# Reordering a top-k attention and mixer kernel: exps ahead of score copies in the second batch, mixing and a last exp moved earlier in the first

## The chip, the cores and the metric

The kernel runs on one core of a Trainium2 chip. The metric is the device time of one execution in microseconds. Three runs of the kernel before took 1866.98, 1867.06 and 1869.12 us, with a median of 1867.06 us; lower is better. The profiled execution of it spans 1865.9 us from its first to its last instruction.

The engines are named as the profile names them: PE is the matrix engine (PEld its weight loads), DVE the vector engine, ACT the scalar engine, POOL the general engine, SP the engine that issues most of the loads and stores.

## The reference

For each of 8 batches and 8 heads, 576 queries attend to 576 keys with head size 64, but only the 32 largest scores of each row are kept. The attention output, with heads side by side, is then the input `x` (576 rows of 512) of a mixer: a low-rank mixing along the sequence, then a two-layer network along the channels.

```python
scores = scale * np.matmul(q, k.transpose(0, 1, 3, 2))
kth = np.partition(scores, -top_k, axis=-1)[..., -top_k:-top_k + 1]
scores = np.where(scores >= kth, scores, -1000000000.0)
attn = np.exp(scores - np.max(scores, axis=-1, keepdims=True))
attn = attn / (np.sum(attn, axis=-1, keepdims=True) + 1e-09)
x = attn @ v                                   # (B, H, S, D) -> (B, S, H*D)

h = x.transpose(0, 2, 1) @ U @ V               # rank 32, along the sequence
u = x + h.transpose(0, 2, 1)
out = u + np.maximum(u @ w_ch1, 0.0) @ w_ch2   # 512 -> 2048 -> 512
```

## The kernel before

Heads are taken in pairs: 4 pairs in a batch, 32 pairs in all. The 576 rows of a pair are cut into four tiles of 128 rows and a tail of 64 rows (both heads of the pair share the tail's tile). A **step** is one tile of one pair, so a pair has 5 steps (`t` = 0 to 4, 4 being the tail), the first batch has steps 0 to 19, the second has steps 20 to 39, and there are 160 steps. Every tile but the tail has two chunks of 128 rows x 576 scores, one for each head; the tail has one.

The order of the instructions on PE, ACT, DVE and POOL is the order in which this program emits them, and each engine works through its own in that order. The program spreads the parts of a step over later steps with Python generators; each `next(...)` emits the part up to the next `yield`.

What becomes of one tile `(g, t)`:

```python
def scores(g, t):              # PE: q times k into PSUM; ACT: three copies out of it into Ssb
    ...
    copy(main[:, :, 0:HALF], scs[0][:, :, 0:HALF])                             # L303
    nc.scalar.copy(main[:, :, HALF:MAIN], scs[1][:, :, 0 : MAIN - HALF])       # L304
    nc.scalar.copy(last, scs[1][:, :, MAIN - HALF : HALF])                     # L305

def front(g, t):               # the top-k and the exps
    ...                        # DVE: first 8 maxima of each chunk (L337)
    yield
    for i in range(1, TOPK // 8):
        if i == 1:
            nc.scalar.mul(nmax[:, 0:n], first[:, 0:n, 0], -SCALE)              # L344
            for c in early:                 # not "eased": exps here already
                weigh(chunks[c], Es[c], nmax[:, c : c + 1])
        ...                    # DVE: match_replace (L349) and max (L353), each chunk
        yield
    if pooled:                 # POOL: scores of chunk 1 under the 32nd get a huge negative number
        nc.gpsimd.tensor_scalar(Es[1], chunks[1], ms[1][:, 7:8], NEG, ALU.is_lt, ALU.mult)   # L356
        nc.gpsimd.tensor_tensor(chunks[1], chunks[1], Es[1], ALU.add)                        # L357
    for c in early:            # DVE: zero what lies under the 32nd, and sum (L359)
        nc.vector.scalar_tensor_tensor(...)
    yield
    if ease:                   # the same for chunk 0 by ACT (L373, L374) and POOL (L375)
        nc.scalar.mul(least, ms[0][:, 7:8], WIDEN)
        nc.scalar.activation(Es[0], chunks[0], AF.Relu, bias=least, scale=-WIDEN)
        nc.gpsimd.tensor_tensor(chunks[0], chunks[0], Es[0], ALU.subtract)
        yield
    for c in order:            # (1, 0)
        if c not in early:
            weigh(chunks[c], Es[c], nmax[:, c : c + 1], sums[c])               # ACT exp, L310
    ...
    yield

def turns(g, t):               # PE transposes E (L395, L400), ACT copies into PT (L396, L401)
def values(g, t):              # PE: PT times v (L429, L432; tail L419), ACT copies into XT (L441)
def mixed(g, wait):            # PE transposes XT, ACT copies to x (L457), POOL divides (L458);
                               # after `wait` calls: PE times U (L464), ACT copies to Tb (L472);
                               # PE times V (L476, L478), ACT copies to uT (L486), in two parts
```

A step is *eased* when `ease` holds: the first two batches' tiles other than tails (and other than step 18). `fill()` emits one call of a `mixed` generator if one is under way, and then a share of the two-layer network's matmuls (`mlp`, PE L501 and L520), once a batch's `mixed` generators are all done; in the first batch there is therefore no such filling. The first batch's steps also decode the parameters (`next_params`: ACT L165 to L168, DVE L175, POOL L176 and L178), and so does the first half of the second batch.

The step loop, second batch and later (`n >= ALONE + 1`; `ease` is that of step n - 1, `last` its generator, `here` that of step n):

```python
        if ease:
            next(last, None)               # least, Relu (ACT), subtract (POOL) of step n - 1
        fill()
        next(turning, None)                # rest of turns(n - 2)
        fill()
        next(turning, None)
        fill()
        next(ready, None)                  # a part of prep: the next pair's q and k
        fill()
        if n - 2 >= ALONE:
            values(*divmod(n - 2, CH))
        if n + 1 < STEPS:
            scores(*divmod(n + 1, CH))
        next(here, None)
        if ease:
            next(last, None)               # the exps of step n - 1
        next_params(1)
        ...
        fill()
        next(here, None)
        fill()
        if n <= STEPS:
            turning = turns(*divmod(n - 1, CH))
        next(turning, None)                # first transposes of step n - 1
```

The loop for the first batch, and for its last step (`ALONE` = 20), stands in the diff below as far as it changes. The whole kernel:

Of the kernel before, what the change touches and what calls it, by code (L numbers as in the profile page):

```python
# [8 lines left out]
F32 = mybir.dt.float32  # L9
# [17 lines left out]
def kernel(  # L27
# [28 lines left out]
    nc = tc.nc  # L56
    B, H, S, D = q.shape
    P = 128
# [4 lines left out]
    NT, TAIL = 4, 64  # L63
    MAIN = NT * P
# [16 lines left out]
    ps_t = ctx.enter_context(tc.tile_pool(name="ps_t", bufs=2, space=bass.MemoryType.PSUM))  # L81
# [9 lines left out]
    ident = const.tile([P, P], F32, name="ident")  # L91
# [30 lines left out]
    def cols(t):  # L122
        return slice(t * P, t * P + rows(t))
# [4 lines left out]
    def half(h):  # L128
        return slice(h * D, (h + 1) * D)
# [120 lines left out]
    def prep(g):  # L250

        tiles, ends = raw.pop(g)
        qkT = attn.tile([P, 2, S], F32, tag="qkT", name="qkT")
        qkTs[g] = qkT
        for i, t in enumerate(tiles):
            tp = ps_t.tile([P, NT, P], F32, tag="tp", name="tp")
            for c in range(NT):
                nc.tensor.transpose(tp[:, c, :], t[:, c].rearrange("p h d -> p (h d)"), ident)  # L258
            copy = nc.vector.tensor_copy if g == 0 and i else nc.scalar.copy
            copy(qkT[:, i, 0:MAIN], tp.rearrange("p t n -> p (t n)"))  # L260
            yield
        tp = ps_t.tile([P, 2, TAIL], F32, tag="tp", name="tp")
        nc.tensor.transpose(
            tp.rearrange("p i n -> p (i n)"), ends.rearrange("p h d -> p (h d)"), ident
        )
        nc.scalar.copy(qkT[:, :, MAIN:S], tp)
        yield

    def scores(g, t):

# [41 lines left out]
    def eased(g, t):  # L312


        return g < 2 * NPAIR and t < NT and (g, t) != (NPAIR - 1, NT - 1)
# [68 lines left out]
    def turns(g, t):  # L384


        E2 = probs.pop((g, t))
        nh = 2 if t < NT else 1
        PT = attn.tile([P, 2 * NT + 1, P], F32, tag="PT", name="PT")
        PTs[g, t] = PT  # L390
        for h in range(nh):
            tp = ps_t.tile([P, NT, P], F32, tag="tp", name="tp")
            for j in range(NT):
                a = h * (S + TAIL) + j * P
                nc.tensor.transpose(tp[:, j, :], E2[:, a : a + P], ident)  # L395
            nc.scalar.copy(PT[:, NT * h : NT * h + NT], tp)  # L396
            yield
        tp = ps_t.tile([P, P], F32, tag="tp", name="tp")
        a = MAIN if nh == 2 else S - P
        nc.tensor.transpose(tp, E2[:, a : a + P], ident)  # L400
        nc.scalar.copy(PT[:, NT * nh], tp)  # L401
        yield

    def inverse(g, lo, hi):
        den = dens[g][:, lo:hi]
        if g == NPAIR - 1:
            nc.vector.tensor_scalar_add(den, den, 1e-9)
        nc.vector.reciprocal(den, den)

    def values(g, t):  # L410

        PT = PTs.pop((g, t))
        va, vd, vt = (a[g % NV] for a in (vas, vds, vts))
        O = ps_t.tile([P, P], F32, tag="tp", name="O")
        if t == NT:
            den, x = dens[g], xs[g % 2]
            inverse(g, 2 * NT if g == NPAIR - 1 else 0, 2 * NT + 1)
            for j in range(NT + 1):
                nc.tensor.matmul(  # L419
                    O,  # L420
                    lhsT=PT[:, j],
                    rhs=va[:, :, j, :] if j < NT else vt,
                    start=(j == 0),
                    stop=(j == NT),
                )
            for h in range(2):
                nc.scalar.mul(x[half(h), NT, half(h)], O[half(h), half(h)], den[half(h), 2 * NT :])
            return
        nc.tensor.matmul(O, lhsT=vd, rhs=PT[:, 2 * NT], start=True, stop=False)  # L429
        for j in range(NT):  # L430
            for h in range(2):
                nc.tensor.matmul(  # L432
                    O[half(h)],
                    lhsT=va[:, h, j, :],
                    rhs=PT[:, NT * h + j],
                    start=False,
                    stop=(j == NT - 1),
                )
        if t == 0:
            XTs[g] = attn.tile([P, MAIN], F32, tag="XT", name="XT")  # L440
        nc.scalar.copy(XTs[g][:, cols(t)], O)  # L441
# [124 lines left out]
    CH = NT + 1  # L566
    STEPS = NP * CH
    ALONE = NPAIR * CH
# [4 lines left out]
    fillers, mixing, due = [], [], 0.0  # L573

    def fill(k=1):

        nonlocal due
        for _ in range(k):
            if mixing and next(mixing[0], True):
                mixing.pop(0)  # L580
            due += share * (SHORT if t == NT else 1) * (EARLY if n <= 2 * ALONE + 2 else 1)
            while due > 0:
                if not fillers:
                    due = 0.0
                    break
                done = next(fillers[0], None)
                if done is None:
                    fillers.pop(0)
                else:
                    due -= done  # L590
# [3 lines left out]
    t = 0  # L594
    for _ in prep(0):
        pass
# [3 lines left out]
    for n in range(STEPS + 2):  # L600
        g, t = divmod(n, CH)
        if n < STEPS:
            if t == 0 and g + 1 < NP:
                load(g + 1)
            if t == 1 and g + 1 < NP:
                ready = prep(g + 1)
            fronts[n] = front(g, t)
            next(fronts[n])
        here, last = fronts.get(n, iter(())), fronts.pop(n - 1, iter(()))
        if n >= ALONE - 1 and n <= ALONE:  # L610

            if n < ALONE:
                values(*divmod(n - 3, CH))
                list(turning)
                scores(*divmod(n + 1, CH))
                values(*divmod(n - 2, CH))
            list(turns(*divmod(n - 1, CH)))
            if n < ALONE:
                next(here)
            values(*divmod(n - 1, CH))  # L620
            if n < ALONE:
                inverse(g, 0, 2 * NT)
                next(here)
                mixing.append(mixed(g, 1))
                fill()
                next(here)
                next(here)
                continue
            fill()
            scores(*divmod(n + 1, CH))  # L630
            next(here)
            while mixing:
# [3 lines that stand above are left out]
            next(last, None)  # L636
            next(here)
            fill()
            next(here)
            next(here)  # L640
            fill()
            continue
        ease = eased(*divmod(n - 1, CH))
        if n < ALONE:
            if ease:
                next(last, None)
            scores(*divmod(n + 1, CH))
            if n >= 3:
                values(*divmod(n - 3, CH))
            list(turning)  # L650
            fill()
            next(here)
            if t < NT:
                next_params(1)
            fill()
            next(ready, None)
            next(here)
            next(last, None)
            fill()
            if n >= 3 and (n - 3) % CH == NT:  # L660
                mixing.append(mixed((n - 3) // CH, 3))
            next(here)
            if t in (0, 1):
                next_params(1)
            next(here)
            fill()
            if n >= 1:
                turning = turns(*divmod(n - 1, CH))
            continue
        if ease:  # L670
            next(last, None)
# [4 lines that stand above are left out]
        fill()  # L676
        next(ready, None)
        fill()
        if n - 2 >= ALONE:
            values(*divmod(n - 2, CH))  # L680
        if n + 1 < STEPS:
            scores(*divmod(n + 1, CH))
        next(here, None)
        if ease:
            next(last, None)
        next_params(1)
        if n - 2 >= ALONE and (n - 2) % CH == NT:
            mixing.append(mixed((n - 2) // CH, 4))
# [8 lines that stand above are left out]
        next(last, None)  # L697
        if t in (1, 3):
# [3 lines that stand above are left out]
# [33 lines left out]
```

## Time and profile before

| | |
|---|---|
| time, median of 3 | 1867.06 us |
| span of the profiled execution | 1865.9 us |
| PE busy | 1747.5 us, 94% |
| PEld busy | 1319.3 us, 71% |
| DVE busy | 1576.7 us, 85% |
| ACT busy | 1009.2 us, 54% |
| POOL busy | 675.0 us, 36% |
| HBM traffic | 58.22 MB by DMA, 31 GB/s on average |

Busy time is summed over the whole span; it tells little of a kernel whose stages differ. The stages are read from the starts of the first maxima on DVE (L337): step 0 begins at 10.9 us, step 20 (second batch) at 213.0 us, step 40 (third batch) at 437.6 us, and the last DVE work of that kind is at 1703 us. A wait in the profile is written as *engine, line that waited <- engine, line that ended the wait*.

### The profile page before, as it was taken

What the parts mean: (1) busy time and instruction counts of PE and PEld (TensorE: products, weight loads), DVE (VectorE), ACT (ScalarE), POOL (GpSimd) and SP (SyncE); (2) the same over time, 40 slices, a digit from 0 to 9 for tenths busy, and PEclk for the clock granted to TensorE, in tenths of its full rate; (3) what the DMA queues carried; (4) which work ended last, traced back from release to release, by engine and by line L of the source; (5) the groups of instructions that cost most, each with busy time, mean ns of one, the idle gap of its engine ahead of it and who ended that gap; (6) DMA issues with size and microseconds to landing.
All of it is one profiled execution on the core that took longest, in us unless ns stands there. A gap on an engine that the chain in (4) does not pass through costs nothing.

```text
span 1865.9 us, 29142 instructions
## 1 busy us (share of the span) xinstructions
PE 1747.5 (94%) x10528; PEld 1319.3 (71%) x10528; DVE 1576.7 (85%) x3224; ACT 1009.2 (54%) x2494; POOL 675.0 (36%) x463
## 2 busy tenths in 40 slices
PE   4665789999999999999999999999999999999999
PEld 2443556677777877788777877788777877778777
DVE  7999988888999999999999999999999989996000
ACT  5777677565545555555555555455555555554111
POOL 4676567433232332323223333332333332322000
PEclk7787899999999999999999999999999999999999
DMA  4222221100001010101001010101001010000000
GB/s 108 76 85 76 60 89 47 28 23 23 24 12 32 23 29 21 26 25 26 16 21 31 21 32 19 28 22 26 14 23 28 25 31 21 9 8 7 6 14 12
DMA packets 127295, 58.22 MB, mean 31 GB/s; under 512 B 89904, under 2 KB 124976, under 8 KB 127152
## 3 DMA queue, kind: packets, MB, share of 16 engines
q1 hardware_dynamic: 126096, 56.10, 11.3%
q8 instruction: 84, 1.38, 0.3%
q14 instruction: 59, 0.48, 0.1%
q10 hardware_dynamic: 1056, 0.26, 0.1%
HBM read 46.89 MB, written 9.44 MB: 30 GB/s over the span
## 4 chain that ended last, share of the span: by engine, by line
PE 84%; DVE 6%; ACT 4%; POOL 3%; issue 2%; DMA 0%; POOLq 0%; SPq 0%; DVEq 0%; ACTq 0%
PE mm L501 26%; PE mm L520 26%; PE sc L292 7%; PE O L432 6%; PE tp L395 6%; DVE rr L349 3%; DVE m L353 2%; PE up L476 2%; PE sc L279 2%; PE O L419 2%; ACT E L310 2%; PE O L429 1%; PE tp L258 1%; PE up L478 1%; PE tp L548 1%
## 5 line engine op out<-in xcount | busy, mean ns | idle before, releaser
L353 DVE MAX8 m<-rr 128x8 f32<-128x576 f32 x864 | 614.6, 748 | 5.5
L520 PE MATMUL mm<-hT,w 128*128 128x256 f32 (+1 forms) x2048 | 563.6, 411 | 0.0
L501 PE MATMUL mm<-uT,w 128*128 128x256 f32 (+1 forms) x2048 | 557.8, 411 | 0.5 <-ACT hT L513 0.5
L356 POOL TENSOR_SCALAR E<-Ssb,m 128x576 f32<-128x576 f32 x127 | 284.7, 2242 | 569.8 <-DVE m L353 409.6
L501 PEld LDWEIGHTS mm<-uT,w 128*128 128x128 f32 x2048 | 363.9, 190 | 107.4 <-issue 28.0
L520 PEld LDWEIGHTS mm<-hT,w 128*128 128x128 f32 x2048 | 361.4, 191 | 98.2 <-issue 23.3
L349 DVE MATCH_REPLACE8 rr<-m,rr 128x576 f32<-128x576 f32 x576 | 427.5, 742 | 0.0
L396 ACT COPY PT<-tp 128x512 f32<-128x512 f32 x288 | 168.4, 587 | 129.1 <-PE tp L395 128.1
L310 ACT ACTIVATE E<-Ssb,nmax 128x576 f32<-128x576 f32 x288 | 222.2, 775 | 14.3 <-POOL Ssb L357 6.2
L395 PE MATMUL tp<-ident,E 128*128 128x128 f32 x1152 | 179.3, 280 | 47.5 <-ACT E L310 24.2
L395 PEld LDWEIGHTS tp<-ident,E 128*128 128x128 f32 x1152 | 140.5, 143 | 102.6 <-ACT E L310 39.7
L337 DVE MAX8 first<-Ssb 128x8 f32<-128x576 f32 x288 | 205.0, 748 | 9.1 <-ACT Ssb L305 8.0
L349 DVE MATCH_REPLACE8 rr<-first,Ssb 128x576 f32<-128x576 f32 x288 | 211.6, 741 | 0.0
L359 DVE SCALAR_TENSOR_TENSOR E<-Ssb,m,E 128x576 f32<-128x576 f32 x130 | 117.1, 901 | 93.5 <-ACT E L310 83.0
L357 POOL TENSOR_TENSOR Ssb<-Ssb,E 128x576 f32<-128x576 f32 x127 | 179.2, 1411 | 10.6
L292 PE MATMUL sc<-qkT 64*128 64x288 f32 x1024 | 169.6, 452 | 8.4 <-ACT Ssb L303 7.9
L513 ACT ACTIVATE hT<-mm 128x320 f32<-128x320 f32 (+1 forms) x256 | 104.1, 407 | 120.0 <-PE mm L501 119.6
L432 PE MATMUL O<-PT,va 128*64 128x128 f32 x2048 | 143.7, 284 | 0.0
L441 ACT COPY XT<-O 128x128 f32<-128x128 f32 x128 | 34.3, 268 | 195.8 <-PE O L432 195.8
L536 POOL TENSOR_TENSOR oT<-oT,uT 128x320 f32<-128x320 f32 (+1 forms) x56 | 45.1, 806 | 230.9 <-ACT oT L535 230.9
L292 PEld LDWEIGHTS sc<-qkT 64*128 64x128 f32 x1024 | 93.0, 197 | 46.1 <-issue 16.6
L432 PEld LDWEIGHTS O<-PT,va 128*64 128x64 f32 x2048 | 112.5, 139 | 16.0 <-issue 1.3
(80 smaller groups left out, 1537.3 us busy)
## 6 DMA issues: line engine op xcount, KB each, us to landing
raw<-in_moe_w_ch_dram SPq DMA_DIRECT2D x32, 512.0 KB, 3.8
va<-in_v_dram SPq DMA_DIRECT2D x64, 128.0 KB, 2.3
out_dram<-ob SPq DMA_DIRECT2D x64, 128.0 KB, 1.9
ld_q<-in_q_dram SPq DMA_DIRECT2D x63, 128.0 KB, 2.8
ld_k<-in_k_dram SPq DMA_DIRECT2D x63, 128.0 KB, 2.8
ld_ends<-in_q_dram SPq DMA_DIRECT2D x32, 32.0 KB, 2.1
ld_ends<-in_k_dram SPq DMA_DIRECT2D x32, 32.0 KB, 2.2
vd<-in_v_dram SPq DMA_DIRECT2D x64, 16.0 KB, 2.0
```

The costliest lines, as they stand in the source:

```text
L292: nc.tensor.matmul(sc[:, h, 0:HALF], lhsT=qkT[half(h), 0, cols(t)], rhs=qkT[half(h), 1, i * HALF : (i + 1) * HALF], start=True, stop=True,)
L310: nc.scalar.activation(E, chunk, AF.Exp, bias=nmax, scale=SCALE, accum_out=total)
L337: nc.vector.max(ms[c], curs[c])
L349: nc.vector.match_replace(nxt, ms[c], curs[c], NEG)
L353: nc.vector.max(ms[c], curs[c])
L356: nc.gpsimd.tensor_scalar(Es[1], chunks[1], ms[1][:, 7:8], NEG, ALU.is_lt, ALU.mult)
L357: nc.gpsimd.tensor_tensor(chunks[1], chunks[1], Es[1], ALU.add)
L395: nc.tensor.transpose(tp[:, j, :], E2[:, a : a + P], ident)
L396: nc.scalar.copy(PT[:, NT * h : NT * h + NT], tp)
L432: nc.tensor.matmul(O[half(h)], lhsT=va[:, h, j, :], rhs=PT[:, NT * h + j], start=False, stop=(j == NT - 1),)
L501: nc.tensor.matmul(ph[:, 0:w], lhsT=w1[:, cc, f * P : (f + 1) * P], rhs=uT[:, cc, lo:hi], start=(cc == 0), stop=(cc == NC - 1),)
L520: nc.tensor.matmul(po[:, 0:w], lhsT=w2[:, f, c * P : (c + 1) * P], rhs=hTs[f][:, 0:w], start=(f == 0), stop=(f == NF - 1),)
```

## The change

There are four moves. No instruction is added or taken away: the 29142 instructions keep their shapes, and only their places in the engines' order change.

1. **First pair's keys and tails.** Before, the transposes for the first scores went q, k, tails; now they go q, tails, k (pair 0 only). It is to free the tails' transposes from the wait for the copy of k.
2. **Mixing in the first batch** begins right after the pair's last `values`, two fills earlier, so that its parts fall into other steps: with the parts of `mixed` numbered by fills, the product with U moves from the third fill of the following step to that step's first, and the two products with V come before the tail's step instead of in it.
3. **The last tail of the first batch** (step 19): its exp is emitted ahead of the transposes of step 18 and the copies after them.
4. **Second batch:** the two exps of step n - 1 are emitted ahead of the copies of `values(n - 2)` and `scores(n + 1)`. It is to let the transposes of step n - 1, which need both exps, start sooner.

```diff
@@ def prep(g)
-        for i, t in enumerate(tiles):
+        for i in (0, 2, 1) if g == 0 else (0, 1, 2):
+            if i == 2:
+                tp = ps_t.tile([P, 2, TAIL], F32, tag="tp", name="tp")
+                nc.tensor.transpose(
+                    tp.rearrange("p i n -> p (i n)"), ends.rearrange("p h d -> p (h d)"), ident
+                )
+                nc.scalar.copy(qkT[:, :, MAIN:S], tp)
+                yield
+                continue
             tp = ps_t.tile([P, NT, P], F32, tag="tp", name="tp")
     (the same lines for the tails taken out below the loop)
@@ step 19
                 scores(*divmod(n + 1, CH))
                 values(*divmod(n - 2, CH))
+                next(here)
             list(turns(*divmod(n - 1, CH)))
-            if n < ALONE:
-                next(here)
             values(*divmod(n - 1, CH))
@@ first batch
             if n >= 3:
                 values(*divmod(n - 3, CH))
+                if (n - 3) % CH == NT:
+                    mixing.append(mixed((n - 3) // CH, 3))
             list(turning)
             fill()
             next(here)
             ...
             next(last, None)
             fill()
-            if n >= 3 and (n - 3) % CH == NT:
-                mixing.append(mixed((n - 3) // CH, 3))
             next(here)
@@ second batch and later
         next(ready, None)
         fill()
+        if ease:
+            next(last, None)
         if n - 2 >= ALONE:
             values(*divmod(n - 2, CH))
         if n + 1 < STEPS:
             scores(*divmod(n + 1, CH))
         next(here, None)
-        if ease:
-            next(last, None)
         next_params(1)
```

More of the change, by code (lines that the diff above doesn't have):

```diff
@@ L254, in prep @@
         qkTs[g] = qkT
-        for i, t in enumerate(tiles):
+        for i in (0, 2, 1) if g == 0 else (0, 1, 2):
[7 more added lines that the diff above has]
+                continue
             tp = ps_t.tile([P, NT, P], F32, tag="tp", name="tp")
             for c in range(NT):
-                nc.tensor.transpose(tp[:, c, :], t[:, c].rearrange("p h d -> p (h d)"), ident)
+                nc.tensor.transpose(tp[:, c, :], tiles[i][:, c].rearrange("p h d -> p (h d)"), ident)
             copy = nc.vector.tensor_copy if g == 0 and i else nc.scalar.copy
@@ L261, in prep @@
             yield
[L262 to L267, printed above, removed]
     def scores(g, t):
```

## The prediction, made before the result was known

> **What bounds the kernel now.** I read the busy times first, then busy time by stage, then the waits of the stage where two engines share the work, then one step of it in the timeline. In the page's first part PE leads, but as an average over stages:
>
> ```profile
> PE 1747.5 (94%) x10528; PEld 1319.3 (71%) x10528; DVE 1576.7 (85%) x3224; ACT 1009.2 (54%) x2494; POOL 675.0 (36%) x463
> ```
>
> The windows cut at the steps' starts (start-up, first batch in two halves, second batch, batches three to eight, tail; the columns are us, then busy us and instructions of each engine, then the granted PE clock, the DMA share and GB/s) show the stages:
>
> ```profile
> 0.00:11.00 11.00, 5.78 (x21) 3.41 (x23) 1.69 (x6) 2.83 (x5) 2.19 (x15) 1.00 0.52 134
> 11.00:109.00 98.00, 58.69 (x328) 38.13 (x328) 96.44 (x197) 67.10 (x163) 64.86 (x50) 0.70 0.31 85
> 109.00:213.00 104.00, 63.83 (x418) 43.55 (x414) 98.82 (x207) 76.64 (x180) 68.00 (x47) 0.79 0.27 79
> 213.00:437.00 224.00, 202.51 (x1217) 147.25 (x1216) 189.36 (x387) 145.18 (x360) 122.93 (x83) 0.98 0.16 44
> 437.00:1710.00 1273.00, 1266.22 (x7878) 968.01 (x7879) 1186.54 (x2426) 692.93 (x1724) 413.77 (x264) 1.00 0.09 22
> 1710.00:1866.00 156.00, 150.50 (x677) 118.91 (x675) 3.85 (x9) 24.53 (x65) 3.22 (x4) 1.00 0.04 12
> ```
>
> The first batch is DVE's: 96.4 of 98 us and 98.8 of 104. From 437 us on PE has 1266.2 of 1273 us, and the change moves nothing there. The second batch belongs to nobody: PE idles 21.5 us of 224 and DVE 34.6. So whatever brings step 40 forward comes out of the total one for one, and nothing else can. The waits between 205 and 440 us (total us, times, longest) say where that stage's idle time lies:
>
> ```profile
> PE tp L395 <- ACT E L310: 15.6, 16, 2.5
> PE pT L464 <- POOL x L458: 3.3, 2, 2.1
> ACT XT L441 <- PE O L432: 23.6, 18, 2.1
> DVE E L359 <- ACT E L310: 17.1, 5, 4.9
> DVE first L337 <- ACT Ssb L305: 7.0, 4, 3.3
> ```
>
> PE's one large wait is for the exps, once for each of the 16 eased steps. ACT meanwhile waits 23.6 us for PE to finish the values. One step shows both on one queue (ACT's timeline; start, duration; idle before and what ended it in brackets):
>
> ```profile
> 368.83 0.26 ACT L266 COPY qkT<-tp 128x128 f32<-128x128 f32 x1
> 370.77 0.27 ACT L441 COPY XT<-O 128x128 f32<-128x128 f32 x1 [1.69 <-PE O L432]
> 371.89 0.64 ACT L286 COPY Ssb<-sc 128x576 f32<-128x576 f32 x1 [0.85 <-PE sc L279]
> 372.43 0.21 ACT L344 ACTIVATE nmax<-first 128x2 f32<-128x2 f32 x1
> 372.53 0.77 ACT L310 ACTIVATE E<-Ssb,nmax 128x576 f32<-128x576 f32 x1
> ```
>
> The inputs of that exp had been ready since 367.4 us, when POOL's subtraction (L375, start 365.95, 1.41 us) ended; it ran at 372.53 because it stood behind the copies, and PE's transposes at 374.21 had idled 0.54 us for it.
>
> **What the Trainium skill says.** "Perfetto Trace Analysis", Optimization Strategy, says that the most contended engine can change between regimes of a kernel, and to look within a regime for that engine's gaps and the semaphore that ends each. The windows agree. "PSUM — Partial Sum Buffer", Engine vs sequencer instructions, says that ScalarE's queue is strictly first in, first out and that matmuls start in program order; the step above agrees, with 5.2 us between the exp's inputs and its start. This cuts both ways: an exp placed early that has to wait for POOL holds up every copy behind it. "TensorE: Matmul & The Clock Gate", What's actually happening, says that idleness throttles PE's clock; the granted clock is 0.70 to 0.79 in the first batch and 0.98 in the second, so denser PE work there may gain a little more than the gaps.
>
> **The change part by part.**
>
> *Start-up.* Before: k's transposes start at 5.53 us, k's copy on DVE ends at 7.34, the tails' transpose has waited for it (7.40), the first scores start at 7.80. The tails' second load is issued at 3.06 us and takes 2.9 us to land, so 5.9. After: tails at about 6.05, k's four transposes take 1.09 us and end near 7.35, copy 0.69 us, scores near 8.1. That is **+0.3 us**: the wait removed is replaced by k waiting for a later load.
>
> *First batch.* DVE waits for a tail's exp (L359) 0.32 us at 108.2, 2.65 at 160.0 and 1.29 at 212.2. In the second case the ACT order is copies of PT, then uT (L486, 0.37 us, after 0.84 us of waiting for PE), then nmax and the exp. The change takes uT and the PE work before it out of the tail's step, and the 1.43 + 0.95 us of the other product with V (148.2 to 150.3 us) out from ahead of that step's scores. I take 2.0 us of the 2.65 and all of the 0.32. At 212.2 the exp moves ahead of three copies (0.59 + 0.59 + 0.27 us) and their waits: all of 1.29. Sum 3.6; I take **-3.3 us**, as ACT's other work moves into the steps before.
>
> *Start of the filling.* The fourth pair's mixing now starts before step 21's scores. Between them stood the chain copy x (0.57), divide on POOL (1.04), and PE waited 2.10 us for it at 220.0 and 0.35 for Tb. The scores (1.24 us) now lie under that chain. **-1.7 us** for the start of the network's matmuls.
>
> *Second batch.* Two exps take 1.6 us and their two accumulator reads 0.2. They now stand where ACT waits for PE's values and scores (1.69 + 0.85 us in the step shown). For each of the 16 steps I compared the end of POOL's L375 with the moment at which ACT would reach the exps. In 12 POOL is done before; in those the copies start 0 to 0.8 us later (once 1.6), and the gap of PE disappears. In four, near 242, 265, 311 and 322 us, POOL is late by 1.4 to 3.5 us, as it also decodes parameters there; the copies then start 1.3 to 4.2 us later. The 16 gaps sum to 15.6 us. Of these the one at 327.3 (2.19) stays, since POOL itself ends it, and about 1.4 us of the others in the first half; 12 us go. Against it: in the four late steps the next score copies, whose results DVE takes 0.9 to 2.6 us after they are made, reach DVE late, and tails' exps behind the moved exps lengthen DVE's wait of 17.1 us. DVE has 34.6 us of idle time to absorb it; I charge 3 us. **-9 us.**
>
> Sum: +0.3 - 3.3 - 1.7 - 9 = -13.7 us. Each us that PE gains also makes it ask for the exps earlier relative to DVE and POOL, so the 2 to 6 us that most steps have spare shrink as the batch goes on. I take three quarters to four fifths of the sum: -11 us, **1856 us**.
>
> **Rivals.**
>
> *ACT held by POOL.* With the exps in front, ACT stalls on L375 and starves DVE of scores. For it: in four steps POOL is late, and over the whole run 6.2 and 3.9 us of ACT's waits before an exp are already for POOL (L357, L375). Against it: the 12 others. If it governs, the second batch gains nothing or loses up to 4 us: about 1862 to 1866.
>
> *DVE becomes the bound of the second batch.* Its work there is 189.4 us; with the 17.1 us for the tails' exps, and perhaps 1.6 us more for each of four tails, that makes about 213 of 224 us. So it does not stop a gain of 9, but it caps it near 11. The time is then 1853 to 1858.
>
> *The first batch's gains are hidden.* If the network's start hangs on something other than DVE's end, only the second batch shows: about 1858. Against it: DVE has no other idle time in that batch, and what starts the network follows step 19's end directly.
>
> **Range and chances.** Full sum and a bonus from the clock: 1849. First rival in part, with the first batch's gain: 1864. PE's idle time before 437 us, less what DVE's own work forces, is no more than some 30 us, so 37 us (2%) are out of reach; and 37 us more would need 2 us of new waiting in each of 20 steps, which nothing in the order suggests. Within 2%: 98%.
>
> **What would show it.** Right: PE's wait for E between 205 and 440 us falls from 15.6 to about 4 us; ACT's wait XT <- O from 23.6 to about 10; DVE's waits of 2.65 and 1.29 us in the first batch are nearly gone; step 20 starts near 210 us instead of 213.0, step 40 near 427 instead of 437.6; the stretch from there to the end keeps its length. Wrong: the wait turns up as ACT E <- POOL Ssb or DVE first <- ACT Ssb; or step 40 comes earlier and the end doesn't; or other steps' DVE gaps grow from the mixing's new places.

## The result, and the profile after

The changed kernel takes 1849.22 us (median of four runs, 1848.58 to 1850.21) against 1867.02 us: 17.8 us less. The ratio of the times is 0.9903, with a 95% interval of 0.9886 to 0.9920. It is a gain well clear of the noise, inside the 2% either way that was forecast, but larger than the 11 us of the prediction and at the lower edge of its range of 1849 to 1864 us (0.9903 of 1867.06 is 1848.9).

The windows of the changed kernel, from 11 us to 1692 us, cut near the starts of its own steps 20 and 40 (209.7 and 421.1 us; columns as before):

```profile
11.00:109.00 98.00, 54.99 (x336) 34.84 (x333) 96.48 (x197) 68.01 (x166) 64.76 (x50) 0.74 0.31 85
109.00:209.00 100.00, 60.27 (x392) 40.94 (x390) 98.12 (x205) 74.99 (x176) 67.97 (x47) 0.78 0.28 82
209.00:420.00 211.00, 199.43 (x1237) 148.42 (x1238) 190.02 (x386) 146.10 (x365) 121.67 (x83) 0.99 0.17 47
420.00:1692.00 1272.00, 1266.59 (x7880) 968.26 (x7879) 1185.89 (x2426) 692.68 (x1723) 412.78 (x264) 1.00 0.09 22
```

The second half of the first batch is 4 us shorter, the second batch 13, and the long stretch after it is as long as it was. In the second batch PE now idles 11.6 us instead of 21.5. The waits there, between 195 and 430 us (total us, times, longest; most line numbers are two higher in the changed kernel, so L359 and L377 are POOL's addition and subtraction):

```profile
DVE E L361 <- ACT E L312: 18.6, 5, 5.9
...
ACT XT L443 <- PE O L434: 10.0, 7, 2.7
ACT E L312 <- POOL Ssb L359: 7.9, 4, 2.9
...
ACT E L312 <- POOL Ssb L377: 3.5, 8, 0.5
...
PE tp L397 <- ACT E L312: 3.4, 3, 1.9
```

PE's wait for the exps fell from 15.6 us in 16 places to 3.4 in three. ACT's wait for the values fell from 23.6 to 10.0, as the exps now run in it; in exchange ACT waits for POOL, 7.9 us in four places (L359) and 3.5 us in eight short ones (L377). The step that the prediction showed, again on ACT's timeline:

```profile
357.08 0.26 ACT L261 COPY qkT<-tp 128x128 f32<-128x128 f32 x1
357.23 0.79 ACT L312 ACTIVATE E<-Ssb,nmax 128x576 f32<-128x576 f32 x1
357.91 0.20 ACT L312 ACTIVATION_READ_ACCUMULATOR E<-Ssb,nmax 128x1 f32 x1
358.00 0.77 ACT L312 ACTIVATE E<-Ssb,nmax 128x576 f32<-128x576 f32 x1
358.67 0.19 ACT L312 ACTIVATION_READ_ACCUMULATOR E<-Ssb,nmax 128x1 f32 x1
359.03 0.27 ACT L443 COPY XT<-O 128x128 f32<-128x128 f32 x1 [0.17 <-PE O L434]
360.15 0.64 ACT L288 COPY Ssb<-sc 128x576 f32<-128x576 f32 x1 [0.85 <-PE sc L281]
```

ACT waited 1.69 us before XT; now the exps fill that, and XT waits 0.17. The score copy still starts when PE's scores end (0.85 us of waiting, as before), so in this step it is not late at all.

A second reading locates the gain more exactly. The network's matmuls come in the same order in both kernels, as 4096 records, so the time of the k-th record is a clock that both share. The first starts at 223.77 us before and at 218.83 after (4.94 us earlier). The 449th, near step 40, starts at 440.15 and 421.29: 18.86 us earlier, so 13.92 us come from the second batch. (The two profiled executions lie 18.86 us apart, the medians of the timed runs 17.8.) From there to the last one it is 1420.87 and 1420.89 us, and between 1420.85 and 1421.55 us in every run below. So what is won by step 40 reaches the end whole.

### The profile page after: what moved, and what is told of

Its sections match the earlier page's. It is cut to its first block, busy times and chain, and to the rows that moved or that the text cites. A ratio compares the mean times of both kernels' runs of the same rounds, so it can differ in the third digit from the quotient of the medians.

```text
span 1847.0 us, 29134 instructions
## 1 busy us (share of the span) xinstructions
PE 1736.2 (94%) x10528; PEld 1314.0 (71%) x10528; DVE 1575.9 (85%) x3224; ACT 1008.3 (55%) x2494; POOL 672.6 (36%) x463
## 4 chain that ended last, share of the span: by engine, by line
PE 84%; DVE 7%; POOL 4%; ACT 3%; issue 1%; DMA 0%; SPq 0%; POOLq 0%; DVEq 0%; ACTq 0%
PE mm L503 26%; PE mm L522 26%; PE sc L294 7%; PE O L434 6%; PE tp L397 6%; DVE rr L351 3%; DVE m L355 3%; PE sc L281 2%; PE O L421 2%; PE up L478 2%; PE O L431 1%; PE tp L266 1%; POOL E L358 1%; PE tp L550 1%; DVE first L339 1%
## 5 line engine op out<-in xcount | busy, mean ns | idle before, releaser
L312 ACT ACTIVATE E<-Ssb,nmax 128x576 f32<-128x576 f32 x288 | 222.8, 776 | 24.3 <-POOL Ssb L359 14.1
L359 POOL TENSOR_TENSOR Ssb<-Ssb,E 128x576 f32<-128x576 f32 x127 | 179.0, 1409 | 10.6
```

The lines of the kernel that those rows point to most:

```text
L312: nc.scalar.activation(E, chunk, AF.Exp, bias=nmax, scale=SCALE, accum_out=total)
```

## Experiments

Times are medians; gains are against the kernel before, on the same chip, with the interval of the ratio turned into us. "Network start" is the start of the network's first matmul.

**Move 4 alone** (the kernel before with the four lines of the second batch's loop changed).

```diff
+        if ease:
+            next(last, None)
         if n - 2 >= ALONE:
             values(*divmod(n - 2, CH))
         if n + 1 < STEPS:
             scores(*divmod(n + 1, CH))
         next(here, None)
-        if ease:
-            next(last, None)
```

> The kernel before with move 4 alone (the second batch's exps ahead of the copies). Theory A (the waits for E are worth their idle time and the restart of PE after each): the network's first matmul stays at 223.8 us, PE's wait tp <- E between 205 and 440 us falls from 15.6 to about 3 us, and the end comes 13 to 14.5 us earlier: about 1853 us. Rival B (the prediction's sizing, late score copies and a shrinking margin eat part of it): 7 to 10 us, 1857 to 1860. Rival C (ACT held by POOL): 1863 to 1867.

1852.04 us: ratio 0.9923 (0.9908 to 0.9937), 14.4 us gained (11.8 to 17.2). PE's waits between 205 and 440 us:

```profile
PE pT L464 <- POOL x L458: 3.8, 2, 2.1
PE tp L395 <- ACT E L310: 2.9, 2, 1.9
```

The wait for E that led this list is down to 2.9 us. From the network's first to its 449th record this run took 201.76 us instead of 216.38. Theory A holds for the gain; the 7 to 10 us of the prediction's sizing, and ACT held by POOL, don't. The network started at 222.4 us in this trace and not at 223.8, although its first batch is that of before; the runs on move 2 come back to that.

**Moves 1 to 3 alone** (the changed kernel with the lines above put back).

> The changed kernel with move 4 undone, so moves 1 to 3 alone. If the first batch's time passes through to the end: the network starts at 218.8 us and the end comes 4 to 6 us earlier than before, 1861 to 1863 us. If it is hidden behind the second batch: 1866 to 1867 us. If the moves depend on each other, the two runs' gains don't add up to 17.8 us.

1863.30 us: ratio 0.9983 (0.9976 to 0.9989), 3.2 us gained (2.1 to 4.5). It passes through to the end, and 14.4 + 3.2 = 17.6 us agrees with the whole gain of 17.8, so there is no sign that the two batches' moves depend on each other, within the some 3 us that the intervals leave open. The gain is below the 4 to 6 us that I expected; the next two runs show how uncertain it is.

**Move 2 undone, and move 3 undone**, each in the changed kernel.

```diff
 # move 2 undone
             values(*divmod(n - 3, CH))
-            if (n - 3) % CH == NT:
-                mixing.append(mixed((n - 3) // CH, 3))
 ...                                # and appended after the second fill again
 # move 3 undone
                 values(*divmod(n - 2, CH))
-                next(here)
             list(turns(*divmod(n - 1, CH)))
+            if n < ALONE:
+                next(here)
```

> The changed kernel with move 2 (mixing begun earlier) undone. If move 2 carries the first batch's gain: step 15 starts 2.5 us later again with DVE's wait E <- E of about 2.6 us back at 160 us, and the network's start comes 3 to 4.5 us later: 1852 to 1854 us. If the last tail's exp (move 3) carried it instead: under 1.5 us later.

> The changed kernel with move 3 (the last tail's exp ahead of the transposes of step 18) undone. If it is worth the wait it was made for: step 20 starts 0.8 to 1.3 us later, and the end as much, about 1850.3 us. If the earlier mixing already takes that wait away: under 0.3 us.

Without move 2: 1854.07 us, 4.4 to 4.9 us later than the changed kernel's two sets of runs (1849.22 and 1849.69). But move 4 alone, which has none of moves 1 to 3, took 1852.04 us. So moves 1 and 3 without move 2 cost 2.0 us, all three together win 2.4 to 2.8 us on top of move 4, and the parts don't add up; why moves 1 and 3 cost time without move 2 stays open.

Without move 3: 1850.19 us, 0.5 to 1.0 us later, which is within the spread of those runs. In its trace DVE waits 3.3 us for the last tail's exp and step 20 starts at 212.57 us, 2.9 us later than in the changed kernel's first trace, but the network starts only 0.8 us later (219.65). So not all that DVE gains there reaches PE.

The waits of DVE in the first batch, from the trace without move 2:

```profile
DVE E L361 <- ACT E L312: 3.8, 3, 2.7
```

The largest of the three is 2.67 us, but at 111.0 us, in the second pair; before, the largest (2.65) was at 160.0, in the third. And in the run with move 4 alone, whose first batch is that of before, the three waits are 0.43, 1.16 and 2.06 us. So a wait for a tail's exp has no fixed size. PE's clock differs with it: in these traces it is granted at half for stretches of multiples of 3.41 us, and they fall elsewhere in each run. ("TensorE: Matmul & The Clock Gate" of the Trainium skill, What's actually happening, has a free-running window of 3413 ns and half the clock after an idle one; the traces agree in both numbers.) At 201 to 208 us the clock's mean is 0.76 in the changed kernel and 0.52 in the run of moves 1 to 3, which have the same first batch:

```profile
201.00:208.00 7.00, 6.83 (x55) 5.15 (x55) 6.70 (x16) 4.21 (x13) 0.00 (x0) 0.76 0.15 51
```

```profile
201.00:208.00 7.00, 6.38 (x33) 5.02 (x35) 6.59 (x17) 3.97 (x12) 0.00 (x0) 0.52 0.24 77
```

PE starts 55 matmul records in the first and 33 in the second (the first number in brackets), and the last tail's wait on DVE is 0.52 and 2.63 us. The other traces with moves 2 and 3 fall in line: with a mean clock of 0.76 in these 7 us the wait is 0.22 to 0.59 us (six traces), with 0.67 it is 1.18, with 0.61 (the changed kernel's second trace) 1.67, with 0.52 2.63. The trace without move 3 has a clock of 0.59 there; by these figures some 1.9 us of its 3.3 would be there with the move too, an estimate that leaves move 3 about 1.4 us of DVE's wait. No run changed the clock by itself, so that it is the whole cause is inferred. The network starts at 223.8 and 222.4 us in the two profiled runs with the old first batch, at 225.6 without move 2, and between 218.4 and 221.1 in the others. Single traces thus give the first batch's gain to no better than 2 us, and the timed 3.2 us is the better figure.

**Tails' steps in the old order** (move 4 undone in the second batch's four tail steps alone).

```diff
-        if ease:
+        if ease and t < NT:
             next(last, None)
 ...
         next(here, None)
+        if ease and t == NT:
+            next(last, None)
```

> The changed kernel with move 4 undone in the second batch's four tail steps alone (there the exps come after the score copies and the tail's exp again). PE's waits for E in those steps were 2.55, 2.19, 1.79 and 2.22 us before. Theory A: three of them come back whole and the fourth (POOL's own) stays, with a restart of PE of about 0.2 us each: 4 to 7 us later than the changed kernel, 1853 to 1856 us, although DVE's wait for the tails' exps (18.6 us) gets shorter by 4 to 8 us. Rival (DVE bounds the second batch): DVE's shorter wait shows, and the time is the same or lower.

1855.48 us, 5.8 to 6.3 us later than the changed kernel. PE's waits between 195 and 430 us begin with

```profile
PE tp L397 <- ACT E L312: 8.7, 5, 2.5
```

that is 5.3 us more than in the changed kernel. DVE's waits in the same window begin with

```profile
DVE E L361 <- ACT E L312: 12.7, 5, 3.9
DVE first L339 <- ACT Ssb L307: 5.4, 4, 2.2
```

The one for the tails' exps got 5.9 us shorter (18.6 in the changed kernel), the one for the scores 4.8 us longer (0.6). The time follows PE's waits and not DVE's wait for the tails.

**More work on DVE** (in the second batch's 16 steps that are not tails, one more maximum whose result nobody uses: 12 us).

```diff
+    junk = const.tile([P, 8], F32, name="junk")
 ...
+        if NPAIR <= g < 2 * NPAIR and t < NT:
+            nc.vector.max(junk, curs[0])
         yield
```

> The changed kernel with one more maximum on DVE, its result unused, in each of the 16 steps of the second batch that are not tails: 16 x 0.75 = 12 us of DVE work. Theory A (PE bounds the second batch and DVE's idle time in the tails' steps absorbs it): DVE's wait for the tails' exps falls by about 3 us each, and the end comes 0 to 5 us later, by the steps where POOL is late. Rival (after the change DVE is the bound): 10 to 12 us later, about 1860 us.

1853.59 us, 3.9 to 4.4 us later: a third of the work added, which is inside the 0 to 5 us expected. DVE's and PE's waits between 195 and 430 us:

```profile
DVE E L364 <- ACT E L313: 14.5, 5, 5.3
```

```profile
PE tp L400 <- ACT E L313: 4.3, 4, 2.0
...
PE pT L469 <- POOL x L463: 2.8, 2, 2.4
PE mm L506 <- ACT hT L518: 2.2, 2, 1.8
```

DVE took a part out of its waits for the tails (18.6 to 14.5 us, less than the 3 us for each tail that were expected). Some of the rest reached PE in small pieces, at the mixing's start and behind ACT. So DVE is not the bound of the second batch, but it isn't far from it.

**Tails' exps first** (in the tail steps, `next(here)` ahead of the two moved exps).

```diff
+        first_tail = ease and t == NT
+        if first_tail:
+            next(here, None)
         if ease:
             next(last, None)
 ...
-        next(here, None)
+        if not first_tail:
+            next(here, None)
```

> The changed kernel with the tail's exp ahead of the two moved exps in the second batch's four tail steps. DVE's wait for it (18.6 us in all between 195 and 430 us) falls to 4 to 8 us. Theory A (DVE's idle time there costs nothing): the end moves by less than 1 us either way. Rival (DVE's tail waits are what limits the second batch now): 5 to 10 us earlier.

1849.94 us, the time of the changed kernel. DVE's waits:

```profile
DVE first L339 <- ACT Ssb L307: 14.0, 6, 3.5
DVE E L361 <- ACT E L312: 1.5, 3, 0.7
```

The 18.6 us of waiting for tails' exps became 1.5, but 14.0 us came up one instruction later, where DVE wants the next step's scores. The wait moved and DVE was hardly freed, so this run doesn't tell the two theories apart; it shows that DVE's wait for a tail is not a need of its own: taken away in one place, it came up in another.

**A spare PSUM buffer at the start** (move 1 replaced: order q, k, tails, with the tails' transposes in the network's pool).

```diff
 ...                                # the loop over q and k, then the tails, as before
+        if g == 0:
+            tp = ps_m.tile([P, C], F32, tag="mm", name="tp")[:, 0 : 2 * TAIL]
+            tp = tp.rearrange("p (i n) -> p i n", i=2)
+        else:
+            tp = ps_t.tile([P, 2, TAIL], F32, tag="tp", name="tp")
```

> The changed kernel with move 1 replaced: the first pair's transposes in the old order q, k, tails, but the tails' go into a PSUM buffer of the network's pool, which is idle then, so that they don't wait for the copy of k. Expected: the first scores start at about 7.4 us (7.80 before, 8.1 in the changed kernel), step 0 at about 10.5 us (10.88 and 11.14), and as the first batch is DVE's, the end 0.6 us earlier than the changed kernel, about 1848.6 us. Rival: the first scores wait for something else (the tails' copy or the loads), and nothing comes earlier than before's 10.88 us.

The first scores start at 7.65 us (8.07 in the changed kernel) and step 0 at 10.71. The end is where it was: 1849.06 us. In this trace step 15 still starts 0.44 us earlier than in the changed kernel's, and step 20 0.2 later, as DVE's wait in the last tail is 1.18 us instead of 0.52. So whether the 0.4 us is there, these runs can't show.

**Decoding behind the masks** (the second batch's decoding at the end of steps 1 and 3 of a pair moves into the next step, behind POOL's subtraction), **all parts joined**, and **the changed kernel again**, on one chip.

```diff
         if ease:
             next(last, None)
+        if t in (2, 4) and n < 2 * ALONE:
+            next_params(1)
 ...
-        if t in (1, 3):
+        if t in (1, 3) and n >= 2 * ALONE:
             next_params(1)
```

> The changed kernel with the second batch's second parameter decoding of a step (at the end of steps 1 and 3 of each pair) moved behind the next step's subtraction on POOL (L377), so that POOL masks a step's scores before it decodes. In the changed kernel PE's waits of the second batch all lie before 320 us, while parameters are decoded: 3.3 us for E and 8.0 us for others. If POOL's decoding ahead of the masks is what makes the exps late there (the prediction's four late steps): PE's waits for E at 262 and 318 us go, with 2 to 4 us off the end, about 1846 us. Rival: ACT's own decoding (2.2 us a time), which moves with it, then delays the copies of PT, PE waits for those instead, and the time stays within 1 us or gets longer.

> All that seemed of use joined: the changed kernel with the spare PSUM buffer at the start, the tails' exps first in the second batch's tail steps, and the decoding behind the masks. If the parts add up: the start 0.4 us and the decoding 2 to 4 us, about 1845.5 us, and DVE's tail waits under 6 us. If the decoding brings nothing: 1848.5 to 1849.5 us.

> The changed kernel itself once more, on the same chip as the two above, so that they can be compared with it: 1848.5 to 1850 us. It also tells how far the first batch's half-clock windows move its parts: the start of step 20 between 209.6 and 212 us.

Decoding later: 1843.54 us. All joined: 1843.11 us (ratio to the kernel before 0.9877, 0.9860 to 0.9893). The changed kernel: 1849.69 us. PE's waits between 195 and 430 us in the first of them:

```profile
PE O L431 <- ACT uT L488: 3.3, 1, 3.3
PE O L431 <- ACT PT L403: 2.6, 2, 2.2
PE pT L466 <- POOL x L460: 2.1, 1, 2.1
...
PE tp L397 <- ACT E L312: 0.2, 1, 0.2
```

The wait for E is 0.2 us, and ACT's wait for POOL's addition fell from 7.9 us to

```profile
ACT E L312 <- POOL Ssb L359: 2.3, 3, 1.5
```

So POOL's decoding ahead of its masks had caused most of the lateness, and taking it away won 6.2 us more, above the 2 to 4 expected (from the network's start to the 449th record, 197.16 us instead of 202.40). ACT's and DVE's part of the decoding moved along, so their share in this gain is not separated. The other two parts add 0.4 us, which lies inside the spread.

## Why the prediction was right and wrong

Two steps failed, both in the size of the second batch's gain. Its sum had no term for the restart of PE after each wait, which the traces put at 2.9 to 3.3 us; and the cut of 2.7 us from the full sum, for margins against POOL that would shrink as PE runs ahead, was for something that hardly happened.

**Where the bound lies: right.** The stretch after step 40 kept its length to 0.1 us in most runs; everything came from before it.

**First batch: right in direction, too large in size.** +0.3 - 3.3 - 1.7 = -4.7 us was forecast for the network's start, and -4.94 was found in the two traces. That agreement is luck: the timed runs give -3.2 us (2.1 to 4.5), or -2.4 to -2.8 on top of move 4. The terms that I read as fixed, 2.65 and 1.29 us of DVE's waiting, were one run's draw, most likely of PE's half-clock stretches. Of the parts, the earlier mixing is needed for the gain (4.4 to 4.9 us are lost without it, more than all three moves win); undoing the last tail's exp moved the time by no more than 1 us. The 0.3 us of the start is seen in the traces (the first scores at 8.07 us, 2.2 us after the tails' last load landed; in the old order at 7.80, 2.4 us after k's last load, which lands some 0.4 us before the tails'), but in the starts of step 0 (10.88 and 11.17 us in the old order, 10.95 to 11.43 in the new) the loads' landing hides it. Move 1 alone was not timed.

**Second batch: the mechanism was right, the sum too small.** -9 us was forecast, and 13.9 was found in the traces (14.4 in the timed runs of move 4 alone). Its parts, from the 1391 matmul records of each trace between the network's start and some way past step 40 (251.2 us before, 237.3 after):

| term | forecast | found |
|---|---|---|
| PE's idle time for E | -12 | -12.3 (15.57 to 3.26) |
| restart of PE after those waits | not seen | -3.3 (exclusive time of the transposes of E: 23.62 to 20.32) |
| given back by late copies | +3, through DVE | +2.3, as other waits of PE (5.7 to 8.0) |
| clock | "a little more" | -0.8 (the first product's matmuls: 70.29 to 69.51; one half-clock stretch fewer after the network's start) |

The four sum to -14.1. The term that was missing is the restart. "Exclusive" is the time of a record that no earlier record covers. A transpose of E that does not wait takes 0.11 us of it in every run, one that waited 0.33 in every run that has such waits. The kernel before shows it on PE's timeline, in a group that did not wait and one that did:

```profile
365.85 0.81 PE L501 MATMUL mm<-uT,w 128*128 128x256 f32 x3
366.50 0.60 PE L395 MATMUL tp<-ident,E 128*128 128x128 f32 x4
366.94 0.60 PE L501 MATMUL mm<-uT,w 128*128 128x256 f32 x2
...
373.07 0.60 PE L501 MATMUL mm<-uT,w 128*128 128x256 f32 x2
374.21 0.66 PE L395 MATMUL tp<-ident,E 128*128 128x128 f32 x4 [0.54 <-ACT E L310]
374.70 0.38 PE L501 MATMUL mm<-uT,w 128*128 128x256 f32 x1
```

The first group starts at 366.50, while the matmuls ahead of it run until 366.66: their tail is covered. The second starts 0.54 us after the matmuls ended (373.67), so it loses those 0.54 us and the overlap besides, about 0.2 us. The ends of PE's records are modelled, but the starts alone say the same: from the start of the last network matmul ahead of the transposes to the start of the first one behind them it is 0.65 us in the first group (366.28 to 366.94) and 1.41 in the second (373.29 to 374.70), 0.76 us more, of which 0.54 are booked as idle. The profile books the other 0.22 as busy; "Perfetto Trace Analysis" of the Trainium skill, Identifying the Most-Contended Engine, warns that PE's busy share is no good measure of how near it is to its peak, as its instructions are pipelined, and here is a case of it. Thirteen waits less at 0.22 us are 2.9 of the 3.3 us in the table; the rest is spread over the transposes that did not wait. The profile's PE busy time, 1747.5 us before and 1736.2 after, holds it, though most of that difference lies in the first batch, where PE's clock is low and its time is free.

**The discount was the other failing step.** I cut -13.7 to -11 us as the margins against POOL would shrink while PE runs ahead. They hardly did. In the step shown POOL's subtraction ended 1.7 us ahead of ACT's reaching the place (367.36 and 369.09), in the kernel before; in the changed kernel, at the same place in the program, it ended at 355.63 (L377, start 354.21, 1.42 us) and the exp ran at 357.23: 1.6 us. Worked out in this way for all 16 steps of the two traces, the margin fell by 0.6 us in the mean: by 1.9 to 2.8 us in three steps, each the first after a tail, and by less than 1 us, or not at all, in the others. It did not go on shrinking: in the last four steps, in which POOL's subtraction came 13 to 17 us earlier than before, it changed by -1.9, -0.2, -0.5 and +0.8 us. PE running earlier makes the scores earlier, so DVE and POOL come along: DVE's wait for scores fell from 8.1 to 0.6 us. The added DVE work shows that this has an end, 4 us of 12, but the change did not reach it.

**Rivals.** *ACT held by POOL* is real (7.9 us in four places, foreseen at the right steps, and 3.5 us in short waits in eight, of which four were not foreseen); decoding later won about 6 us while relieving it, but it didn't eat the gain. *DVE as the bound* is refuted by the added work, of which two thirds cost nothing, and by the tails' steps; the cap of 11 us that I put on the gain from it was wrong: the 17.1 us of DVE's tail waits that I counted as DVE's own need are left-over time, since a wait that was taken away came up again elsewhere. *Hidden first batch* is refuted by moves 1 to 3 alone.

**What would show it.** Forecast and found: PE's wait for E about 4 us, 3.4; ACT's wait for the values about 10, 10.0; step 20 near 210, 209.7; step 40 near 427, 421.1. The last of these was the miss. DVE's waits in the first batch were nearly gone in the first trace (0.5 us), but 1.7 and 2.6 us in two others with the same first batch. One of my signs of being wrong, ACT's wait for POOL, did turn up, and the gain was larger than forecast all the same: as far as these runs show, a wait of ACT costs what reaches PE of it.

## What to carry to other kernels

On an engine that works strictly in order, put work whose inputs are ready ahead of work that waits for another engine; it then runs in that wait, and costs the later work little (nothing in the step shown). When sizing the gain, count a restart of PE for each wait removed, beside the idle time, and don't take the idle time of a partner that follows the bound as that partner's own need. An order that works only when a third engine is on time shows where to look next: here it was POOL's decoding ahead of its masks, worth a third of the change's gain again.

## What the runs showed of the hardware

A transpose of 128x128 in fp32 after a wait of PE takes 0.33 us that no earlier record covers, instead of 0.11; the mean is the same to 0.004 us in the eleven traces that have such waits. Half-clock stretches of PE come in multiples of 3.41 us at places that differ from run to run, in a stage where PE idles by a third and more; the start of the next stage differed by up to 2.7 us between runs of the same order of instructions, and DVE's last wait before it was the longer the lower the clock.
